# Moving the memory-value transfers ahead of a unit's values, and halving the dummy products of block 0

## The chip, the cores and the metric

The kernel runs on one core of one Trainium2 chip. The metric is the device time of one launch in microseconds (us). A core has five engines with their own instruction queues that run in program order: TensorE (PE in the profile, its weight loads PEld), VectorE (DVE), ScalarE (ACT), GpSimd (POOL) and SyncE (SP). In this kernel SP does nothing but issue DMA transfers, one after another.

## The reference, cut to what matters

Chunked attention with memory slots, then two multi-layer perceptrons on its output (3072 tokens of width 512):

```python
for c in range(nc):                      # chunks of 32 queries, per batch and head
    k_full = concat([mem_k, k_ctx])      # 8 memory keys and a window of 16 + 32 + 8
    v_full = concat([mem_v, v_ctx])
    a = softmax(scale * q_c @ k_full.T)
    out[:, :, c_start:c_end] = a @ v_full
x = out as (tokens, 512)
h = max(max(x @ w1, x @ w2), x @ w3);  x = h @ w_out        # first perceptron
h = x @ w_in;  g = where(h >= 1, h, where(h <= -1, 0, (h + 1) ** 2 / 4))
out = g @ w_out2                                             # second perceptron
```

Four batches, 8 heads, 768 positions, 8 memory slots, head width 64.

## The kernel before, in words

Attention is cut into 24 units of 128 queries, all heads at once; six units (UPB) make one batch, so units 0, 6, 12 and 18 begin a batch. Of a unit `u` the steps are: `s` scores on PE (line 379), `mx`, `ex`, `n` softmax on DVE and ACT (393, 394, 398, 402 to 405), `a` transpose of the probabilities on PE (411), `ca` copy to `aT` (415), `o` product with the values on PE (427), `cx` and `dx` split of the result into a rounded half `xh` (ACT, 437) and a rest `xl` (DVE, 441). The output product `o` of unit `u` is issued at the start of unit `u+1`, just ahead of that unit's scores.

The values of a unit lie in a tile `vw` of 128 rows: two halves of 64, each with 8 rows of memory values and 56 rows of the window, for four chunks. From unit 5 on there is one buffer. `load_v` (`lv`, line 266) fills the window rows with eight transfers from HBM. `fill_mv` (`mv`, line 255) fills the memory rows with two transfers from the small tile `mv`, once in each batch; `load_mv` (`lm`, line 248) brings that tile from HBM one batch ahead. Every transfer is issued by SP, and `mv` and `lv` of unit `u` both have to wait until `o` of unit `u-1` has read `vw`.

Tokens form six blocks of 512 (four units). Block 0 follows an order written out by hand, the string `PLAN`: attention of the first nine units, preparation of the weights (`f`, `wa` to `ws`) and the first perceptron's products for block 0 (`l`, `lt`, `lh`, `m`). A word `d3`, `d6` or `d7` in it is a call of `warm`: four products of the identity with itself into a bank that nobody reads (line 1012). Nothing on another engine waits for them; they stand in PE's queue in their places.

From then on a generator `steps(u)` yields six steps for each unit, and one step is issued beside each group of twelve or twenty-four 512-column products of the first perceptron (lines 500 to 502, the copy and maxima at 533 and 535, the split at 517 and 519). Step 1 is `o, s, cx, mx, dx, ex`; step 2 `n, lv`; step 3 transposes of keys and queries for later units by DVE (`fk` 356 and 357, `fq` 364) and the making of a list of their transfers, which `feed` then issues a few at a time (line 941); step 4 `a, ca`; step 5, until now, `mv`; step 6 `lm`. The steps of `PLAN` reach into unit 8, so that of the batch beginnings only units 12 and 18 go through the generator.

The same loop prepares the second perceptron's weights, by part of a unit (`round_step`): a fetch of 1 MB in two transfers (120 or 122), conversion on ACT and DVE (135 to 162, 176 to 179) and stores to HBM (949 to 953, 955 and 956). They share the SP queue with the units' values, in program order.

Of the kernel before, what the change touches and what calls it, by code (L numbers as in the profile page):

```python
# [37 lines left out]


PLAN = """  # L40
d3 lk1 d3 lmem0 d3 d3 lk0 d3 lm0 d3 d3 lq0 lv1 tk1 mem0 ck1 tk0 d3 ck0 ek1 tq0 lk2 kw0 d3 mv2 d3 d3
cq0 lq1 lk3 s0 mv0 mx0 lq2 tk2 mv1 d3 ck2 ek2 lk4 tq1 ex0 lv0 d3 cq1 n0 tk3 kw1 d3 ck3 s1 ek3 a0 kw2
mx1 tq2 lq3 tk4 cq2 f0 ck4 f1 s2 ex1 lk5 f2 d3 ek4 mx2 d3 f3 kw3 d3 lq4 lv2 ca0 n1 tq3 ex2 o0 cq3 n2
a1 cx0 s3 ca1 d7 dx0 wa0 mx3 o1 wr0 tk5 wc0 a2 cx1 d7 d7 ca2 d7 ex3 d7 dx1 ck5 d7 d7 ek5 wd0 d3 kw4
d3 n3 wa1 tq4 f4 d3 cq4 lv3 wc1 wr1 s4 wh0 o2 kw5 wd1 a3 d7 cx2 d7 ws0 f5 wh1 d7 lq5 d7 f6 dx2 ca3
d7 f7 mx4 lk7 o3 lv4 ws1 ex4 d7 cx3 d7 n4 d7 wa2 d6 tq5 wr2 dx3 a4 d6 wc2 cq5 ca4 s5 l0 wa3 wd2 wr3
mx5 f9 l1 f8 wh2 lv5 wc3 ex5 lt0 o4 n5 l2 cx4 lt1 ws2 lq7 a5 lq6 wd3 ca5 l3 lm1 wa4 dx4 lk6 f11 lt2
wr4 f10 wc4 l4 lh2 lt3 wh3 wd4 tq7 o5 cq7 ws3 f13 wh4 f12 tk6 mv6 l5 cx5 ws4 lk8 ck6 lv6 dx5 wa5 lt4
tq6 lt5 wr5 m0 wc5 cq6 lh5 wa6 l6 wd5 wr6 wc6 lq8 f14 wh5 f15 tk7 l7 lt6 lk9 ck7 ws5 ek7 kw6 wd6 l8
lt7 f16 wh6 f17 ws6 s6 lt8 wa7 m1 mx6 wr7 wc7 lh8 ex6 tq8 l9 cq8 wa8 wd7 m2 wr8 wc8 f18 f19 lt9 wh7  # L50
l10 wd8 ws7 f21 wh8 f20 n6 tk8 l11 ck8 ek8 lt10 kw7 ws8 wa9 tk9 lt11 l12 wr9 wc9 ck9 wa10 a6 lh11
wd9 l13 ek9 wr10 f22 f23 wc10 ca6 lt12 m3 wh9 wd10 o6 ws9 wh10 s7 lt13 cx6 lv7 ws10 wa11 l14 mx7
wr11 kw8 dx6 l15 lq10 lt14 ex7 lk10 wc11 lk11 lh14 lm2 lq9 l16 lt15 wd11 m4 n7 wh11 ws11 a7 lt16 l17
ca7 o7 lt17 lh17 s8 cx7 dx7 m5 mx8 ex8 f24 f25 f26 f27
""".split()

ON_DVE = """
# [8 lines left out]
def attention_then_two_mlps(ctx, tc, q, k, v, mem_k, mem_v, w1, w2, w3, w_mid, w_in, w_out, out):  # L66
# [8 lines left out]
    UPB = S // P  # L75
# [375 lines left out]
    def steps(u):  # L451
        old = u + 1 < TRIO0
        late = not old and u % 3 == 2
        if u == UB:
            yield [("s", u), ("mx", u), ("ex", u)]
        else:
            yield [("o", u - 1), ("s", u), ("cx", u - 1), ("mx", u), ("dx", u - 1), ("ex", u)]
        m = [("n", u), ("lv", u)]
        if old:
            v = [("tk", u + 2), ("ck", u + 2), ("ek", u + 2)] if u + 2 < TRIO0 else []  # L460
            v += [("lk", u + 4)] if u + 4 < TRIO0 else []
            yield m + v + [("kw", u + 1)]
            v = [("tq", u + 1), ("cq", u + 1)]
            v += [("lq", u + 3)] if u + 3 < TRIO0 else []
        else:
            yield m
            v = [("fk", u + 1)] * (not late)
        if u + 2 >= TRIO0:
            v += [("fq", u + 2)]
        if u == TRIO0 - 3 or u >= TRIO0 - 2 and u % 2 == 0:  # L470
            v += [("gq", u // 2 + 2)]
        if u >= TRIO0 - 2 and u % 3 == 1:
            v += [("gk", u // 3 + 1)]
        yield v
        yield [("a", u), ("ca", u)]
        new = u % UPB == 0
        yield [("mv", u)] * new + [("fk", u + 1)] * late
        yield [("lm", u // UPB + 1)] if new else []
        if u == NU - 1:
            yield [("o", u), ("cx", u), ("dx", u)]  # L480
# [3 lines left out]
    def run(kind, i):  # L484
# [3 lines left out]
        elif kind in WEIGHTS or i < NU:  # L488
            parts[kind](i)

    todo = [s for u in range(UB, NU) for s in steps(u)]
    todo.reverse()

# [386 lines left out]
    def last_evict(p):  # L880

        for i in range(2):
# [10 lines left out]
            nc.sync.dma_start(out=out[r0:r0 + 2 * P, HK:].rearrange("(t p) d -> p t d", p=P), in_=o)  # L893

    def pair_l4(p, steps):

        last = p + 1 == NB // 2
# [79 lines left out]
    with tc.manual_schedule(engines={ENG.PE, ENG.DVE, ENG.Activation, ENG.Pool, ENG.SP}):  # L977
# [56 lines left out]
        for j in range(1, NB):  # L1034
            for f in range(K1):
                l2 = [(slot_l2, *((j, f - 1) if f else (j - 1, K1 - 1)))] if j > 1 or f else []
# [154 lines left out]
```

## Time and profile before

| | |
|---|---|
| median of 3 runs | 979.41 us (979.38 to 980.14) |
| the profiled execution | 980.73 us, of which 979.0 us are the span of its instructions |
| PE busy | 952.9 us, 97% of the span |
| DVE, ACT, POOL busy | 72%, 55%, 35% |
| chain that ended last | PE 92%, DVE 3%, DMA 1%, SP's queue 1%, unexplained issue 1% |
| granted clock of TensorE, mean | 0.987 of full speed |

The span is the time from the first to the last instruction of one profiled execution. The granted clock is the share of TensorE's full clock (2.4 GHz) that the chip allowed; its lower level, 0.50, is 1.2 GHz. "issue" in the chain and among the waits is time in which an engine waited for nothing that the profile can name.

### The profile page before, as it was taken

To read this page: it belongs to the slowest core of one execution; us is meant where nothing else is said; L and a number is where in the kernel's file an instruction comes from. 1 tells how busy PE (TensorE), PEld (TensorE's weight loads), DVE (VectorE), ACT (ScalarE), POOL (GpSimd) and SP (SyncE) were. 2 spreads that over 40 slices of the span, in tenths; PEclk is the share of its full clock that TensorE was granted. 3 is DMA by queue.
4 is the path that set the end of the run, shared out by engine and by line. 5 is a ranking of instruction groups with operands and counts; after the bars stand their busy time and mean duration, and the time that the engine had idled before them with its cause. 6 is when DMAs were issued, how large, how long until landed. Compare 5 with 4: busy or idle time off the path is not lost.

```text
span 979.0 us, 19063 instructions
## 1 busy us (share of the span) xinstructions
PE 952.9 (97%) x7166; PEld 784.7 (80%) x7166; DVE 704.9 (72%) x1001; ACT 541.3 (55%) x972; POOL 339.0 (35%) x330
## 2 busy tenths in 40 slices
PE   7899999997999989999999999999999999999998
PEld 6788877886888868888888888888888888888886
DVE  2899947584776757762427777998777998777855
ACT  4766644342334223232338777776777776776763
POOL 0000002221221011111456665555655554665552
PEclk8999999998999989999999999999999999999999
DMA  7796546657677567435224226534225734323723
GB/s 173 214 230 198 159 130 159 161 146 196 183 216 191 139 167 213 148 100 188 75 72 141 85 83 224 178 109 103 92 76 153 267 113 97 87 87 97 258 65 64
DMA packets 242779, 142.81 MB, mean 146 GB/s; under 512 B 174464, under 2 KB 210176, under 8 KB 242688
## 3 DMA queue, kind: packets, MB, share of 16 engines
q1 hardware_dynamic: 242688, 141.60, 50.7%
q8 instruction: 56, 0.92, 0.4%
q14 instruction: 35, 0.29, 0.1%
HBM read 109.71 MB, written 31.46 MB: 144 GB/s over the span
## 4 chain that ended last, share of the span: by engine, by line
PE 92%; DVE 3%; DMA 1%; SPq 1%; issue 1%; ACT 1%; POOL 0%; POOLq 0%; ACTq 0%; DVEq 0%
PE psums L500 29%; PE psums L502 28%; PE psums L501 28%; PE psums L427 3%; PE psums L379 2%; PE psums L411 1%; DMA kq<-in_q_dram 1%; PE psums L1012 0%; PE psums L305 0%; PE psums L274 0%; DVE c L151 0%; SPq L941 0%; DMA vw<-mv 0%; SPq L255 0%; DVE lo L205 0%
## 5 line engine op out<-in xcount | busy, mean ns | idle before, releaser
L519 POOL TENSOR_TENSOR hl_a<-t,hh_a 128x512 fp32r<-128x512 f32 x30 | 41.4, 1380 | 398.7 <-ACT hh_a L517 387.8
L500 PE MATMUL psums<-xh,hi 128*128 128x512 f32 x432 | 173.4, 401 | 0.0
L502 PE MATMUL psums<-xh,lo 128*128 128x512 f32 x432 | 169.6, 392 | 0.0
L501 PE MATMUL psums<-xl,hi 128*128 128x512 f32 x432 | 169.3, 392 | 0.2 <-DVE xl L441 0.2
L810 POOL TENSOR_TENSOR hb<-h,hb 128x512 fp32r<-128x512 f32 x72 | 99.4, 1381 | 92.6 <-PE psums L502 59.8
L802 ACT CAST hb<-h 128x512 fp32r<-128x512 f32 x144 | 88.8, 622 | 48.1 <-PE psums L501 46.5
L535 DVE TENSOR_TENSOR t<-psums,t 128x512 f32<-128x512 f32 x72 | 49.5, 687 | 69.8 <-PE psums L502 69.8
L502 PEld LDWEIGHTS psums<-xh,lo 128*128 128x128 f32 x432 | 81.7, 189 | 18.5 <-DVE lo L205 0.9
L630 POOL TENSOR_TENSOR hb<-ra,hb 128x256 fp32r<-128x256 f32 x96 | 75.2, 796 | 58.9 <-ACT hb L629 55.6
L500 PEld LDWEIGHTS psums<-xh,hi 128*128 128x128 f32 x432 | 81.8, 189 | 16.8 <-issue 0.3
L501 PEld LDWEIGHTS psums<-xl,hi 128*128 128x128 f32 x432 | 82.0, 190 | 16.5 <-DVE xl L441 0.6
L694 ACT ACTIVATE psums<-h 128x512 f32<-128x512 f32 x96 | 57.9, 603 | 60.4 <-DVE h L780 24.2
L502 PE MATMUL psums<-t,hb 128*128 128x512 f32 x192 | 74.8, 390 | 0.0
L501 PE MATMUL psums<-t,hb 128*128 128x512 f32 x192 | 74.7, 389 | 0.0
L500 PE MATMUL psums<-t,hb 128*128 128x512 f32 x192 | 74.7, 389 | 0.0
L630 POOL TENSOR_TENSOR hb<-rb,hb 128x256 fp32r<-128x256 f32 x72 | 55.4, 775 | 39.5 <-ACT hb L629 39.5
L808 DVE TENSOR_TENSOR hb<-psums,hb 128x512 fp32r<-128x512 f32 x66 | 44.9, 680 | 24.8 <-PE psums L502 20.6
L500 PE MATMUL psums<-hh_a,hi 128*128 128x512 f32 x144 | 57.4, 399 | 1.3 <-ACT xh L437 1.3
L437 ACT CAST xh<-psums 128x512 fp32r<-128x512 f32 x24 | 14.0, 585 | 79.8 <-PE psums L379 50.9
L695 ACT ACTIVATE psums<-psums 128x512 f32<-128x512 f32 x96 | 55.9, 582 | 3.1
L833 DVE TENSOR_TENSOR h<-h,h 128x1024 f32<-128x1024 f32 (+1 forms) x42 | 56.5, 1368 | 0.0
L502 PE MATMUL psums<-hh_a,lo 128*128 128x512 f32 x144 | 56.2, 390 | 0.0
(145 smaller groups left out, 2301.0 us busy)
## 6 DMA issues: line engine op xcount, KB each, us to landing
t<-td SPq DMA_DIRECT2D x15, 1024.0 KB
ra<-cd SPq DMA_DIRECT2D x24, 512.0 KB
st<-in_moe_w_out_dram SPq DMA_DIRECT2D x22, 512.0 KB
st<-in_moe_w_dram SPq DMA_DIRECT2D x18, 512.0 KB
vw<-in_v_dram SPq DMA_DIRECT2D x152, 56.0 KB
st<-in_moe_w_in_dram SPq DMA_DIRECT2D x16, 512.0 KB
h<-yd SPq DMA_DIRECT2D x12, 512.0 KB
rb<-cd SPq DMA_DIRECT2D x24, 256.0 KB
```

The costliest lines, as they stand in the source:

```text
L500: nc.tensor.matmul(out, whi, xhi, start=first, stop=False)
L501: nc.tensor.matmul(out, whi, xlo, start=False, stop=False)
L502: nc.tensor.matmul(out, wlo, xhi, start=False, stop=last)
L519: e.tensor_tensor(out=lo, in0=h, in1=hi.bitcast(F32), op=ALU.subtract)
L535: nc.vector.tensor_tensor(out=cur["t", j, f], in0=s, in1=cur["t", j, f], op=ALU.max)
L630: nc.gpsimd.tensor_tensor(out=c[:, 1], in0=t, in1=c[:, 0].bitcast(F32), op=ALU.subtract)
L694: nc.scalar.activation(out=a, in_=x, func=AF.Relu, bias=0.5, scale=0.5)
L695: nc.scalar.activation(out=a, in_=a, func=AF.Square)
L802: nc.scalar.copy(out=hi, in_=x)
L808: nc.vector.tensor_tensor(out=lo, in0=y, in1=hi.bitcast(F32), op=ALU.subtract)
L810: nc.gpsimd.tensor_tensor(out=lo, in0=x, in1=hi.bitcast(F32), op=ALU.subtract)
L833: nc.vector.tensor_tensor(out=x, in0=y, in1=z, op=op)
```

## The change

Two edits. In `steps`, the word `mv` of a unit that begins a batch moves from step 5 to step 2, between `n` and `lv`: its two transfers are now issued ahead of the eight of `lv` and not after the transfers that `feed` and the weight stores issue in steps 3 and 4. Nothing else of the generator changes; for units 12 and 18 the issue order on SP differs, and on no other engine.

In `PLAN`, 19 of the 37 words `d` are left out, with four products each: 76 of 148. What stays: five before the first key transpose, one before `s0` (`kw0 d3 mv2 cq0 lq1 lk3 s0`), one after `s2`, six around `ca2 ex3 dx1 ck5 ek5`, three after `a3`, two after `o3`. All other words keep their order. Among those left out are the ones between `tk0` and `tq0`, between `tk2` and `tq1`, `tq1` and `tk3`, `tk3` and `s1`, two of three after `s2`, the one between `s3` and `o1`, and the one between `a4` and `s5`.

```diff
 PLAN = """
-d3 lk1 d3 lmem0 d3 d3 lk0 d3 lm0 d3 d3 lq0 lv1 tk1 mem0 ck1 tk0 d3 ck0 ek1 tq0 lk2 kw0 d3 mv2 d3 d3
-cq0 lq1 lk3 s0 mv0 mx0 lq2 tk2 mv1 d3 ck2 ek2 lk4 tq1 ex0 lv0 d3 cq1 n0 tk3 kw1 d3 ck3 s1 ek3 a0 kw2
-mx1 tq2 lq3 tk4 cq2 f0 ck4 f1 s2 ex1 lk5 f2 d3 ek4 mx2 d3 f3 kw3 d3 lq4 lv2 ca0 n1 tq3 ex2 o0 cq3 n2
-a1 cx0 s3 ca1 d7 dx0 wa0 mx3 o1 wr0 tk5 wc0 a2 cx1 d7 d7 ca2 d7 ex3 d7 dx1 ck5 d7 d7 ek5 wd0 d3 kw4
...
+d3 lk1 d3 lmem0 d3 d3 lk0 d3 lm0 lq0 lv1 tk1 mem0 ck1 tk0 ck0 ek1 tq0 lk2 kw0 d3 mv2 cq0 lq1 lk3 s0
+mv0 mx0 lq2 tk2 mv1 ck2 ek2 lk4 tq1 ex0 lv0 cq1 n0 tk3 kw1 ck3 s1 ek3 a0 kw2 mx1 tq2 lq3 tk4 cq2 f0
+ck4 f1 s2 ex1 lk5 f2 d3 ek4 mx2 f3 kw3 lq4 lv2 ca0 n1 tq3 ex2 o0 cq3 n2 a1 cx0 s3 ca1 dx0 wa0 mx3 o1
+wr0 tk5 wc0 a2 cx1 d7 d7 ca2 d7 ex3 d7 dx1 ck5 d7 d7 ek5 wd0 kw4 n3 wa1 tq4 f4 cq4 lv3 wc1 wr1 s4
...
-        m = [("n", u), ("lv", u)]
+        m = [("n", u)] + [("mv", u)] * (u % UPB == 0) + [("lv", u)]
...
-        yield [("mv", u)] * new + [("fk", u + 1)] * late
+        yield [("fk", u + 1)] * late
```

## Rows read from the trace of the kernel before

**Rows 1.** The page: busy us of each engine, share, instructions

```profile
PE 952.9 (97%) x7166; PEld 784.7 (80%) x7166; DVE 704.9 (72%) x1001; ACT 541.3 (55%) x972; POOL 339.0 (35%) x330
```

**Rows 2.** Waits of PE, 60 to 450 us: total us, times, longest

```profile
PE psums L427 <- issue: 9.2, 2, 4.7
PE psums L500 <- ACT xh L437: 1.3, 1, 1.3
```

**Rows 3.** Chain that ended last, 205 to 235 us: start us, us, what

```profile
223.76 2.48 DMA vw<-mv
226.29 1.93 PE psums L427 x62
```

**Rows 4.** The same chain over the whole span, units 12 to 19

```profile
212.49 0.44 PE psums L411 x4
...
239.47 0.44 PE psums L411 x4
...
258.35 0.44 PE psums L411 x4
...
266.98 1.06 PE psums L427 x64
...
333.90 0.44 PE psums L411 x4
...
359.86 0.44 PE psums L411 x4
```

**Rows 5.** Timeline of SP: start us, us, line, transfer, count

```profile
207.81 5.52 SPq L266 DMA_DIRECT2D vw<-in_v_dram  x8
...
222.97 1.47 SPq L255 DMA_DIRECT2D vw<-mv  x2
...
232.24 4.47 SPq L266 DMA_DIRECT2D vw<-in_v_dram  x8
238.71 4.92 SPq L941 DMA_DIRECT2D kq<-in_k_dram  x10
...
251.21 0.89 SPq L120 DMA_DIRECT2D st<-in_moe_w_out_dram  x2
...
254.59 6.22 SPq L266 DMA_DIRECT2D vw<-in_v_dram  x8
...
332.72 4.87 SPq L266 DMA_DIRECT2D vw<-in_v_dram  x8
...
343.50 1.68 SPq L255 DMA_DIRECT2D vw<-mv  x2
```

**Rows 6.** Timelines of ACT and DVE in unit 14

```profile
259.31 1.12 ACT L135 ACTIVATE c<-st 128x1024 f32<-128x1024 f32 x1
...
263.67 0.70 DVE L356 STREAM_TRANSPOSE kw<-kq 128x512 f32<-128x512 f32 x1
```

**Rows 7.** Groups of PE by line, 0 to 50.6 us: busy us, mean ns, idle before

```profile
L1012 PE MATMUL psums<-ident 128*128 128x256 bf16 x148 | 20.9, 296 | 1.4 <-POOL ident masks.py:199 1.4
```

**Rows 8.** Chain that ended last, 0 to 60 us

```profile
16.84 0.85 PE psums L1012 x4
...
23.48 1.42 PE psums L1012 x12
...
26.18 1.93 issue
...
48.13 0.70 DVE p L405
...
49.53 0.44 PE psums L1012 x4
```

**Rows 9.** By stretch: us, busy us of PE, PEld, DVE, ACT, POOL; granted clock; DMA

```profile
28.00:32.00 4.00, 3.89 (x103) 2.96 (x104) 2.34 (x5) 2.50 (x4) 0.00 (x0) 0.57 1.05 273
...
44.00:48.00 4.00, 3.39 (x85) 3.00 (x84) 3.90 (x7) 2.47 (x4) 0.00 (x0) 1.00 1.06 316
...
120.00:140.00 20.00, 18.71 (x210) 15.16 (x209) 8.62 (x14) 8.90 (x16) 0.00 (x0) 1.00 0.47 155
```

More of the change, by code (lines that the diff above doesn't have):

```diff
@@ L40 @@
 PLAN = """
-d3 lk1 d3 lmem0 d3 d3 lk0 d3 lm0 d3 d3 lq0 lv1 tk1 mem0 ck1 tk0 d3 ck0 ek1 tq0 lk2 kw0 d3 mv2 d3 d3
-cq0 lq1 lk3 s0 mv0 mx0 lq2 tk2 mv1 d3 ck2 ek2 lk4 tq1 ex0 lv0 d3 cq1 n0 tk3 kw1 d3 ck3 s1 ek3 a0 kw2
-mx1 tq2 lq3 tk4 cq2 f0 ck4 f1 s2 ex1 lk5 f2 d3 ek4 mx2 d3 f3 kw3 d3 lq4 lv2 ca0 n1 tq3 ex2 o0 cq3 n2
-a1 cx0 s3 ca1 d7 dx0 wa0 mx3 o1 wr0 tk5 wc0 a2 cx1 d7 d7 ca2 d7 ex3 d7 dx1 ck5 d7 d7 ek5 wd0 d3 kw4
-d3 n3 wa1 tq4 f4 d3 cq4 lv3 wc1 wr1 s4 wh0 o2 kw5 wd1 a3 d7 cx2 d7 ws0 f5 wh1 d7 lq5 d7 f6 dx2 ca3
@@ L46 @@
[L46 to L54, printed above, removed]
+d3 lk1 d3 lmem0 d3 d3 lk0 d3 lm0 lq0 lv1 tk1 mem0 ck1 tk0 ck0 ek1 tq0 lk2 kw0 d3 mv2 cq0 lq1 lk3 s0
+mv0 mx0 lq2 tk2 mv1 ck2 ek2 lk4 tq1 ex0 lv0 cq1 n0 tk3 kw1 ck3 s1 ek3 a0 kw2 mx1 tq2 lq3 tk4 cq2 f0
@@ new lines @@
+ck4 f1 s2 ex1 lk5 f2 d3 ek4 mx2 f3 kw3 lq4 lv2 ca0 n1 tq3 ex2 o0 cq3 n2 a1 cx0 s3 ca1 dx0 wa0 mx3 o1
+wr0 tk5 wc0 a2 cx1 d7 d7 ca2 d7 ex3 d7 dx1 ck5 d7 d7 ek5 wd0 kw4 n3 wa1 tq4 f4 cq4 lv3 wc1 wr1 s4
+wh0 o2 kw5 wd1 a3 d7 cx2 d7 ws0 f5 wh1 d7 lq5 f6 dx2 ca3 f7 mx4 lk7 o3 lv4 ws1 ex4 d7 cx3 d7 n4 wa2
+tq5 wr2 dx3 a4 wc2 cq5 ca4 s5 l0 wa3 wd2 wr3 mx5 f9 l1 f8 wh2 lv5 wc3 ex5 lt0 o4 n5 l2 cx4 lt1 ws2
+lq7 a5 lq6 wd3 ca5 l3 lm1 wa4 dx4 lk6 f11 lt2 wr4 f10 wc4 l4 lh2 lt3 wh3 wd4 tq7 o5 cq7 ws3 f13 wh4
@@ new lines @@
+f12 tk6 mv6 l5 cx5 ws4 lk8 ck6 lv6 dx5 wa5 lt4 tq6 lt5 wr5 m0 wc5 cq6 lh5 wa6 l6 wd5 wr6 wc6 lq8 f14
+wh5 f15 tk7 l7 lt6 lk9 ck7 ws5 ek7 kw6 wd6 l8 lt7 f16 wh6 f17 ws6 s6 lt8 wa7 m1 mx6 wr7 wc7 lh8 ex6
+tq8 l9 cq8 wa8 wd7 m2 wr8 wc8 f18 f19 lt9 wh7 l10 wd8 ws7 f21 wh8 f20 n6 tk8 l11 ck8 ek8 lt10 kw7
+ws8 wa9 tk9 lt11 l12 wr9 wc9 ck9 wa10 a6 lh11 wd9 l13 ek9 wr10 f22 f23 wc10 ca6 lt12 m3 wh9 wd10 o6
+ws9 wh10 s7 lt13 cx6 lv7 ws10 wa11 l14 mx7 wr11 kw8 dx6 l15 lq10 lt14 ex7 lk10 wc11 lk11 lh14 lm2
@@ L55 @@
+lq9 l16 lt15 wd11 m4 n7 wh11 ws11 a7 lt16 l17 ca7 o7 lt17 lh17 s8 cx7 dx7 m5 mx8 ex8 f24 f25 f26 f27
 """.split()
```

## The prediction

> **What bounds the kernel now.** I read the page first: PE is busy 97% of the span [rows 1], so a change counts only where it takes away PE time or a wait of PE. Next the waits of PE. Between block 0's beginning and the end of attention nearly all of them belong to one line, the output product at 427: 9.2 us in two waits [rows 2], which the profile cannot name itself ("issue"). Then the chain of waits around the first one. It says what released PE: a transfer `vw<-mv`, issued at 223.76, landed 2.48 later, at 226.24, and the product runs from 226.29 [rows 3]. That is `o` of unit 12, waiting for the memory rows of its value tile. SP's timeline says why they came late: their two issues stand at 222.97, behind feeds and weight stores, while the unit's eight value transfers were issued at 207.81 [rows 5]. Unit 18 repeats the pattern: values at 332.72, memory rows at 343.50 [rows 5].
>
> What a stall costs in all I take from the period of the units, measured from one transpose `a` to the next: undisturbed 258.35 - 239.47 = 18.88 us; over the first stall 239.47 - 212.49 = 26.98; over the second 359.86 - 333.90 = 25.96 [rows 4]. The excess is 8.10 and 7.08, 15.18 together, of which 9.2 are idle; the other 6.0, about 3.0 for each, is PE running slowly afterwards (the product took 1.93 [rows 3] where an ordinary one takes 1.06 [rows 4]).
>
> **The move, part by part.** It adds and removes no instruction. Two issues of 1.47 us in all (1.68 in unit 18) [rows 5] go ahead of the eight value issues.
>
> *Unit 12.* An ordinary `o` starts 266.98 - 258.35 = 8.63 us after `a` [rows 4], so `o` of unit 12 is due at 212.49 + 8.63 = 221.12. Its values' last issue ends at 207.81 + 5.52 + 1.47 = 214.80 at the latest. From the end of an issue to landing I take 226.24 - (222.97 + 1.47) = 1.8 [rows 3, 5]. That gives 216.6: 4.5 us to spare, and the memory rows are earlier still. *Unit 18:* due at 333.90 + 8.63 = 342.53; values issued by 332.72 + 4.87 + 1.68 = 339.27, landed 341.1: 1.4 to spare. Both stalls should go, and with them the slow stretch behind each: -15.18. What waits behind the moved issues on SP (feeds, stores) is later by at most 1.5 to 1.7 us, until the place that the pair left; from there SP is where it was.
>
> *What is late next.* PE reaches units 13 and 14 8.10 us sooner, but SP does not. It is almost never idle from 207.81 to the end of unit 14's values at 254.59 + 6.22 = 260.81 [rows 5]. Unit 13: `o` due at 239.47 - 8.10 + 8.63 = 240.0; values end at 232.24 + 4.47 = 236.71 as before, landed 238.5: hidden, by 1.5. Unit 14: `o` due at 266.98 - 8.10 = 258.88. If SP gains nothing, the values land at 260.81 + 1.8 = 262.6, 3.7 late. SP gains at least the hole between 236.71 and 238.71 [rows 5], which is a wait for DVE's transposes to free the key buffer, and those come with PE, 8 us sooner. With 2.0 gained they land at 260.6, 1.7 late; the pair's old place may give back another half. Bounds 0 (SP gains more than I can see) and 3.7; I take 1.5, near the row of the hole.
>
> In the same unit the fetch at 251.21 moves only those 2 us, while ACT's conversion at 259.31, which needs it, is due at 251.2. That conversion delays DVE, and the key transpose at 263.67 stands behind it [rows 5, 6]. How late the conversion gets depends on the fetch's landing, of which the rows give bounds alone: 1.8 after its issue ends at 250.1 (0.7 late) and 2.0 before the conversion ran, at 257.3 (6.1 late). The key transposes (two of 0.70, to 265.1) were done 2.9 us before the scores that need them, at 266.98 + 1.06 = 268.04 [rows 4, 6]. With the 1.5 already counted, 4.4 us of delay stay hidden, the middle of the bounds (3.4) among them: I add 0, with 1.7 as the other end.
>
> A second stall of 1.5 us could also drop the clock. Against that stands a wait of 1.3 us for `xh` [rows 2]; it is the 1.29 us that PE is not busy in 120 to 140 us, where the clock stayed at 1.00 [rows 9]. I take no drop.
>
> **The dummy products.** 76 of 148 go. At the full clock four of them take 0.44 [rows 8], so 8.4 us of PE time leave the first 50 us (20.9 for all [rows 7]). Little of that is on the path. The chain holds none before 16.84: up to there it runs through SP and DMA. Then it holds two groups of 0.85 (one stands in rows 8), two thirds of 1.42 at 23.48, both ahead of a 1.93 issue stall at 26.18, and 0.44 at 49.53 [rows 8]; one more group lies in the slow stretch after the stall. From about 35 to 48.8 the chain is on ACT and DVE, and late in it DVE is busy 3.90 of 4.00 us [rows 9]; the transpose `a` of unit 4 waits for DVE's softmax, which ends at 48.83 [rows 8], whatever PE did before. Behind it only the last group is a plain saving, 0.44, of which the ACT copy of unit 5's queries, just ahead of its scores, leaves about 0.2. The earlier groups, 0.85 + 0.85 + 0.95 = 2.65, help only as far as they let DVE begin that busy stretch sooner; the stall at 26.18 and ACT's copies stand between. Bounds 0 and 2.65; I count none, since a stall that PE itself did not cause is the nearest row.
>
> What the dummies hid: without them PE idles between the small attention products, and the clock can fall. The rows show that it does in this stretch: after the 1.93 us of waiting at 26.18 [rows 8] the granted clock in 28 to 32 is 0.57, a mix of 0.50 and 1.00, while 44 to 48, with dummies, is at 1.00 [rows 9]. If it is at 0.50 when block 0's first large product starts, at about 50.5, the price is what the slow stretches of units 12 and 18 cost, 3.0. At half clock earlier than that, PE's small products have DVE's busy stretch to hide behind. Eighteen of the 37 groups remain, among them eleven between 34 and 47 us, so I take 0 here and keep 3.0 for the range. The Trainium skill, TensorE: Matmul & The Clock Gate, in its section on what is actually happening, says that the low clock is the default and that activity releases it; its section on oscillation says that waits between bursts of products bring it back. By that rule the half that is left out would cost the 3.0 and the sum would be three less; the trace agrees with the rule at 28 to 32 us but does not show whether the remaining half is enough.
>
> **The sum.** -15.18 (two stalls) + 1.5 (unit 14's values) + 0 (conversion) - 0.2 (last dummy group) + 0 (clock) = -13.9. The profiled execution took 980.73 for a span of 979.0 and would take 966.8. The median of the runs, 979.41, is 1.32 below it, so the median becomes 979.41 - 13.9 = 965.5. After 450 us nothing changes: PE runs without waits, and what it feeds shifts with it.
>
> **The rivals.** (A) As summed: 961.6 to 968, chance 0.62. (B) SP takes back more: unit 14's values are 3.7 late, and the idle time halves the clock (3.0): 6.7 given back in place of 1.5, 970.7; the conversion's 1.7 would lie within the same wait. For it speaks that SP has hardly a hole for 50 us; against it, that one hole is a wait that vanishes. The milder form, 1.5 and the clock, is 968.5. Chance 0.15. (C) The clock is at half at block 0's first large products: +3.0, 968.5; for and against as above; chance 0.13. (D) The change doesn't do what it says: what held `o` of units 12 and 18 was something behind the memory rows and as late, and the wait keeps its length under another name: about 979.2. Against it stands the landing at 226.24 and the start 0.05 later [rows 3]; for it, that the profile itself calls most of the waiting "issue" [rows 2]. Chance 0.05. (E) Slower: the clock stays at 0.50 well into block 0. Each slow stretch of units 12 and 18 cost about 3.0 us before the clock was back [rows 2, 4]; the 13.9 are used up only by nearly five such stretches on end, and from there it decides: six give 979.41 - 13.9 + 18 = 983.5. Nothing in the trace comes near. Chance 0.02. (F) The dummies' 2.65 and no give-back: 979.41 - 15.18 - 2.65 = 961.6; chance 0.03.
>
> **The numbers.** This kernel's runs tell about 0.2% (2 us) from no change. Faster by more than that are A, B, C and F: 0.93; within it D: 0.05; slower E: 0.02. The range goes from F's 961.5 to 972.0, past B: all but D, E and a remainder.
>
> **What would show it right or wrong.** Right: no wait at line 427 near 221 or 335; the transposes of units 12 and 13, and 18 and 19, 18.9 apart; a wait of 1 to 2 us at 427 near 259 with the clock at 1.00; transpose `a` of unit 4 still released by DVE near 48.8; clock 1.00 from 50 us on. Wrong: a clock of 0.50 at 50 to 54 us (C); a wait above 2 us near 259 and 0.50 behind it, or waits in unit 15 too (B); waits of 4 us left at 427 in units 12 and 18 (D); block 0's first large product two or more us sooner than 50.7 (F).

## The result, and the profile after

The changed kernel took 969.03 us (median of 4 runs, 967.93 to 969.68), the kernel before 979.39 (median of 4, 977.88 to 980.14) beside it on the same chip: ratio 0.9895 [0.9878, 0.9912], 10.4 us faster. The prediction was 965.5 with a range of 961.5 to 972.0, so the median lies inside it. The profiled execution took 968.48 us for a span of 966.7, so against the profile of before the span is 12.3 us shorter, where 13.9 were forecast.

In the code after, line numbers are one lower than before (`o` is 426, `a` 410, the scores 378, the first perceptron's products 499 to 501, the copy `t` 532, the conversion 134, the fetch 119).

The page after, busy us of each engine, answers to [rows 1]:

```profile
PE 945.5 (98%) x7090; PEld 777.7 (80%) x7090; DVE 705.2 (73%) x1001; ACT 542.2 (56%) x972; POOL 339.5 (35%) x330
```

PE has its 76 dummy instructions less and nothing else changed in count. Waits of PE after, 60 to 450 us, answer to [rows 2]: total us, times, longest.

```profile
PE psums L499 <- ACT t L532: 3.3, 1, 3.3
...
```

The two waits of `o`, 9.2 us together, are gone, and so is the one of 1.3 for `xh`. Below what the fence shows come 0.8 and 0.2. A wait stands there that [rows 2] did not have: a large product waits 3.3 us for ACT's copy `t`. The chain that ended last, transposes `a` of units 12 to 16 and the stretch of that wait, answers to [rows 4]:

```profile
210.23 0.44 PE psums L410 x4
...
229.11 0.44 PE psums L410 x4
...
256.62 1.06 PE psums L426 x64
...
266.87 0.44 PE psums L410 x4
...
270.90 3.58 DMA vw<-in_v_dram
274.48 1.13 ACT st L138
275.60 0.47 ACT t L532
276.12 0.61 PE psums L499
276.73 0.43 PE psums L500
...
291.00 0.44 PE psums L410 x4
```

Unit 12 now takes 229.11 - 210.23 = 18.88 us, an undisturbed period, where it took 26.98: 8.10 gained. Unit 15 takes 291.00 - 266.87 = 24.13, 5.25 more than undisturbed: 3.3 of waiting, and the rest at half clock (granted 0.59 and 0.56 in 276 to 278 and 278 to 280 us), for the products behind the wait take 0.43 us each instead of the usual 0.23. The chain puts a value transfer ahead of ACT's second conversion step (274.48). That is an inference from times that coincide: the step reads and writes `st` alone, and in ACT's timeline below the wait stands ahead of the first step, where the landing of the fetch ends it. Further down the same chain unit 18 is undisturbed too:

```profile
328.76 0.44 PE psums L410 x4
...
347.64 0.44 PE psums L410 x4
```

18.88 again, where it was 25.96: 7.08 gained. So the shifts of `a` against the profile of before are -2.26 from block 0 and the wait for `xh` (210.23 against 212.49), -10.36 behind unit 12, -5.13 behind unit 15 (291.00 against 296.13 for unit 16), -12.22 behind unit 18, and nothing afterwards.

SP's timeline after shows why ACT was late in unit 15; it answers to [rows 5]. Columns: start us, us, line, transfer, count.

```profile
204.60 1.46 SPq L254 DMA_DIRECT2D vw<-mv  x2
206.10 5.39 SPq L265 DMA_DIRECT2D vw<-in_v_dram  x8
...
229.04 4.74 SPq L265 DMA_DIRECT2D vw<-in_v_dram  x8
233.88 4.96 SPq L940 DMA_DIRECT2D kq<-in_k_dram  x10
...
249.47 4.98 SPq L265 DMA_DIRECT2D vw<-in_v_dram  x8
...
264.05 3.93 SPq L352 DMA_DIRECT2D kT<-in_q_dram  x6
268.09 0.87 SPq L119 DMA_DIRECT2D st<-in_moe_w_out_dram  x2
```

And ACT's timeline after, units 14 (as [rows 6]) and 15; in brackets the idle time ahead and what ended it:

```profile
251.44 1.12 ACT L134 ACTIVATE c<-st 128x1024 f32<-128x1024 f32 x1 [2.39 <-DMA st<-in_moe_w_out_dram]
...
267.35 0.59 ACT L414 COPY aT<-psums 128x512 f32<-128x512 f32 x1 [3.52 <-PE psums L410]
267.83 0.62 ACT L516 CAST hh_a<-t 128x512 fp32r<-128x512 f32 x1
273.45 1.13 ACT L134 ACTIVATE c<-st 128x1024 f32<-128x1024 f32 x1 [5.00 <-DMA st<-in_moe_w_out_dram]
274.47 1.14 ACT L138 ACTIVATE st<-st 128x1024 uint32<-128x1024 uint32 x1
275.50 0.57 ACT L532 COPY t<-psums 128x512 f32<-128x512 f32 x1
```

The fetch of unit 15's weights is issued at 268.09, behind the flush of the transposed queries (264.05), with no gap on SP. ACT reaches the conversion right behind 267.83, stands still for 5.00 us until `st` has landed, and the copy `t`, which needs nothing of that fetch, is queued behind the two conversion steps. PE's large products take turns in two PSUM banks, and it needs the one that `t` empties.

Of block 0, the windows by stretch answer to [rows 9] (us, busy us of PE, PEld, DVE, ACT, POOL; granted clock; DMA share, GB/s):

```profile
44.00:48.00 4.00, 3.43 (x19) 2.13 (x17) 3.90 (x7) 3.69 (x5) 0.00 (x0) 0.53 1.06 327
48.00:52.00 4.00, 4.00 (x74) 3.27 (x74) 3.84 (x6) 3.37 (x4) 0.00 (x0) 0.61 0.85 162
52.00:56.00 4.00, 4.00 (x41) 3.10 (x39) 3.86 (x7) 1.62 (x3) 0.00 (x0) 1.00 0.85 276
```

and the chain that ended last, from 41 us on, answers to [rows 8]:

```profile
41.05 4.82 DMA kq<-in_q_dram
...
45.91 1.11 PE psums L304 x4
47.03 1.02 PE psums L410 x4
...
49.16 0.72 PE psums L499
```

Transpose `a` of unit 4 starts at 47.03 here, where the softmax that it waited for in [rows 8] ended at 48.83, and no longer waits for it: PE comes to it straight from the transposes of unit 5's queries (line 304), which waited for those queries until 45.87. The clock fell to 0.50 at about 44.2 us and was back from about 51.

### The profile page after: what moved, and what is told of

It reads as the page before. It is cut to its first block, busy times and chain, and to the rows that moved or that the text cites. A ratio compares the mean times of both kernels' runs of the same rounds, so it can differ in the third digit from the quotient of the medians.

```text
span 966.7 us, 18906 instructions
## 1 busy us (share of the span) xinstructions
PE 945.5 (98%) x7090; PEld 777.7 (80%) x7090; DVE 705.2 (73%) x1001; ACT 542.2 (56%) x972; POOL 339.5 (35%) x330
## 4 chain that ended last, share of the span: by engine, by line
PE 93%; DVE 2%; DMA 2%; SPq 1%; ACT 1%; issue 1%; POOL 0%; POOLq 0%; DVEq 0%; ACTq 0%
PE psums L499 29%; PE psums L501 28%; PE psums L500 28%; PE psums L426 2%; PE psums L378 2%; PE psums L410 1%; PE psums L273 1%; DMA kq<-in_k_dram 1%; DMA kq<-in_q_dram 0%; PE psums L304 0%; PE psums L1011 0%; DMA vw<-in_v_dram 0%; SPq L360 0%; SPq L265 0%; SPq L940 0%
## 5 line engine op out<-in xcount | busy, mean ns | idle before, releaser
L500 PE MATMUL psums<-hl_a,hi 128*128 128x512 f32 x144 | 56.2, 390 | 0.0
```

The lines of the kernel that those rows point to most:

```text
L500: nc.tensor.matmul(out, whi, xlo, start=False, stop=False)
```

## The experiments

Each ratio is against the kernel before, run beside it on the same chip; those medians of before were 977.52 (the first four kernels), 977.34 (e5 to e8) and 975.94 (e9 to e12).

| | median us | ratio, interval |
|---|---|---|
| e1 the move alone | 967.16 | 0.9890 [0.9873, 0.9906] |
| e2 the halved dummies alone | 974.96 | 0.9967 [0.9951, 0.9983] |
| e3 both, conversion of unit 15 a step later | 965.34 | 0.9869 [0.9846, 0.9892] |
| e4 both, three of the late dummy groups put back | 965.35 | 0.9864 [0.9841, 0.9886] |
| e6 the change again | 967.29 | 0.9911 [0.9883, 0.9939] |
| e7 both, stores and fetch ahead of the feeds in a step | 968.94 | 0.9920 [0.9891, 0.9948] |
| e9 both, fetch right behind the stores | 976.27 | 1.0005 [0.9983, 1.0027] |
| e10 as e4, conversion a step later in all units | 963.22 | 0.9869 [0.9839, 0.9899] |
| e11 as e4, fetch earlier and conversion later | 978.32 | 1.0034 [1.0010, 1.0057] |
| e12 the move, no dummy at all | 962.31 | 0.9866 [0.9831, 0.9901] |

e5 (before, 979.17) and e8 (967.84) ran once each, for their traces. By these intervals e3, e4, e10 and e12 can't be told from each other, and e3 and e4 touch those of the change (0.9895 and, in e6, 0.9911): what single waits are worth is read from the traces.

**The two edits alone.** e1 has the edit of `steps`, e2 the new `PLAN`, nothing else.

```diff
 # e1
-        m = [("n", u), ("lv", u)]
+        m = [("n", u)] + [("mv", u)] * (u % UPB == 0) + [("lv", u)]
-        yield [("mv", u)] * new + [("fk", u + 1)] * late
+        yield [("fk", u + 1)] * late
 # e2: only the words "d" of PLAN that the change leaves out
```

> The move alone, all 148 dummy products kept. Theory: the two edits add up, and the move brings the two stalls (15.2 us) less what unit 15 gives back where ACT's conversion waits for the weight fetch (5.2 in the profile of the changed kernel): about 10 faster than before, with a wait of PE of about 3 us for the copy t in unit 15. Rival: the give-back comes only because the halved dummies let PE run 2 us further ahead of SP; then unit 15 shows less than half of that wait, and the move alone brings 13 or more.

> Only the dummy products halved, the move undone. Theory: DVE's busy stretch in block 0 begins about 2 us sooner, and after the first 140 us the trace stands about 2.2 us ahead of before; the stalls of units 12 and 18 remain, since their end is set by SP's queue, but the first of them begins sooner, so that part of the 2.2 is lost to it if SP does not move: 0 to 2.2 faster. Rival (my prediction): 0.2 faster, within what can be told from none; and the 2.2 of the profile is the scatter of early DMA traffic.

e1 gains 10.36 us and e2 2.56, which add up to 12.9; the whole change gained 10.4 (and 10.1 when it was run again, e6). The 2.5 between them are no more than the intervals leave open, but the traces agree that the two take something from each other. Waits of PE in e1, 60 to 450 us:

```profile
PE psums L500 <- ACT xh L437: 1.0, 1, 1.0
...
```

The next are 0.8 and 0.2, and none is for `t`: with the old `PLAN` PE comes to unit 15 at 270.82, 3.95 later than after the change, while SP issues the fetch at 268.65, only 0.56 later. So of e1's theory the size came true and the reason did not: unit 15 gives back 0.14 us in place of 5.2, as the rival had it, and yet the gain is 10.36 and not 13. Part of that is the smaller stalls of the next paragraph: of e5's 12.6 us, 0.14 go in unit 15 and 0.64 before unit 8 (141.18 against 140.54), which leaves the 11.8 that lie between the spans of e5 and e1 (977.4 and 965.6). In e2 both waits of `o` are there (`L426 <- issue` 8.5 in two), so the dummies have nothing to do with the stalls.

**How large the stalls are: the kernel before once more (e5), and the change once more (e6), no edit.**

> The kernel before, profiled a second time. Theory: the first 60 us (small products between early transfers, with a clock that falls and rises) differ from execution to execution by some us, the two stalls of units 12 and 18 do not; so the excess of the two disturbed periods is again 8.1 and 7.1 within 0.5, and what differs between the two profiles lies before 140 us. Rival: the stalls themselves vary, which is why the median gained less than the trace shows; then one of them is shorter by 2 us or more.

> The changed kernel again, on the chip and in the rounds of the next two. Theory: the wait for the copy t in unit 15 is there again (3 us, and 5 in all with the clock); the clock at 44 to 51 us may stand at either level, since a kernel with the same dummies showed 1.00 there. Rival: the wait in unit 15 was chance, and its loss comes out under 2 us.

ACT's copies of `a` for units 12, 13 and then 18, 19 in e5 (start, us):

```profile
214.06 0.58 ACT L415 COPY aT<-psums 128x512 f32<-128x512 f32 x1 [2.52 <-PE psums L411]
236.88 0.58 ACT L415 COPY aT<-psums 128x512 f32<-128x512 f32 x1 [5.75 <-PE psums L411]
...
331.29 0.58 ACT L415 COPY aT<-psums 128x512 f32<-128x512 f32 x1 [2.52 <-PE psums L411]
358.85 0.59 ACT L415 COPY aT<-psums 128x512 f32<-128x512 f32 x1 [7.69 <-PE psums L411]
```

Unit 12 exceeds the 18.88 of an undisturbed unit by 3.94 here and unit 18 by 8.68: 12.6 together, against 15.18 in the profile that the prediction used. In e2, which has the same stalls, it is 232.34 - 208.92 - 18.88 = 4.54 and 354.55 - 327.07 - 18.88 = 8.60, 13.1 together. The first number of the sum was thus one draw, and the largest of three, as e5's rival had it. e6 repeats the loss of unit 15 (5.17 in place of 5.25, the wait for `t` 3.3 again), so that one is no accident; it adds 1.65 in unit 19, with another wait for `t`, of 1.4.

**Is it the order within the step?** e8 keeps the move to step 2 but issues the memory rows behind the eight value transfers.

```diff
-        m = [("n", u)] + [("mv", u)] * (u % UPB == 0) + [("lv", u)]
+        m = [("n", u), ("lv", u)] + [("mv", u)] * (u % UPB == 0)
```

> The changed kernel with the memory rows behind the unit's eight value transfers, still in step 2. Theory: what counts is that they no longer stand behind feeds and stores; they land by 217 in unit 12 and 341 in unit 18, before the product is due: no wait, periods of 18.9 us as in the changed kernel. Rival: the order within the step matters, and a wait of 1 us or more is left in unit 18, where my margin was 1.4 us.

The stalls are gone as well; a wait of 0.3 for `vw<-mv` is left at line 426, in unit 18, well under the 1 us of the rival. What counts is the distance to the feeds and stores of steps 3 and 4, not which of the two goes first.

**Conversion later.** In e3 ACT's conversion (`"a"`) of unit 15 alone is issued one step later, behind the copies `t` of the step where it blocked; in e10 that of every unit, together with three dummy groups put back as in e4.

```diff
 # e3
+                if done == 45:
+                    acts.remove("a")
+                if done == 46:
+                    acts.insert(0, "a")
 # e10
-    BY_PART = "", "p", "", "out a", "in in", "b"
+    BY_PART = "", "p", "", "out", "a in in", "b"
-                round_step(BY_PART[part].split() + (["a"] if s == 1 else []))
+                round_step(BY_PART[part].split())
```

> The changed kernel, with the conversion that waits 5 us for its fetch in unit 15 put one step (3.1 us of products) later, behind the copy t that PE needs. Theory (the conversion blocks ACT's queue, and PE waits for the copy behind it, not for the weights): the wait of 3.3 us for t goes, and the slow clock behind it: 3 to 5.2 us faster than the changed kernel. Rival (PE was held by DVE or by a bank that the late fetch holds in another way): the wait stays at 3 us under another name, no change.

> The version with the last three dummy groups back, and the conversion one step later in every unit. Theory: no wait for t above 1 us in units 15, 19 and 20, the gain of the move is kept whole: about 12 to 14 faster than before. Rival: the later conversion makes the stores or DVE's combining late, and waits of PE turn up elsewhere; no better than the version with the dummies alone.

ACT's timeline of e3 in unit 15:

```profile
266.52 0.59 ACT L414 COPY aT<-psums 128x512 f32<-128x512 f32 x1 [5.10 <-PE psums L410]
...
269.32 0.59 ACT L532 COPY t<-psums 128x512 f32<-128x512 f32 x1 [1.70 <-PE psums L501]
270.43 1.12 ACT L134 ACTIVATE c<-st 128x1024 f32<-128x1024 f32 x1 [0.52 <-DMA st<-in_moe_w_out_dram]
```

The copy runs ahead of the conversion, as soon as PE has the product; no wait at `t` is left in unit 15, and one of 0.8 for `xl` of DVE has come up there, probably since the later conversion delays DVE. From unit 15 to 16 that is 286.53 - 266.52 = 20.01 between ACT's copies of `a`, 1.13 over the undisturbed 18.88 and not 5.25: 4.1 gained there. e10 has no wait for `t` left from 60 to 450 us; one for `xl` (1.3, at 204 us) is the largest. Its unit 15 loses 0.45, where e4, with the same dummies and the conversion in its old place, loses 1.90. Both ratios are 0.9869, and e4's is 0.9864: the traces of unit 15 show what the later conversion does, the medians don't show it by themselves.

**Fetch earlier on SP.** If the conversion waits for the fetch, the fetch could come first. e7 has stores and fetch issued ahead of the feeds of the same step, e9 the fetch in the step of the stores, e11 that and the later conversion.

```diff
 # e7
-                feed((5, 6, 4, 6, 5, 1)[part])
                 round_step(BY_PART[part].split() + (["a"] if s == 1 else []))
+                feed((5, 6, 4, 6, 5, 1)[part])
 # e9: as e7, and
-    BY_PART = "", "p", "", "out a", "in in", "b"
+    BY_PART = "", "p", "", "out a in in", "", "b"
 # e11: round_step ahead of feed and without the "a" of s == 1, dummies as e4, and
+    BY_PART = "", "p", "", "out in in", "a", "b"
```

> The changed kernel with the weight stores and fetches issued in each step ahead of the feed transfers instead of behind them. Theory (SP's order makes the fetch late, not the transfer itself): the fetch of unit 14 is issued 2 to 5 us sooner against PE, ACT's wait of 5.0 us in unit 15 shrinks below 2, PE's wait for t goes: 3 to 5 faster than the changed kernel. Rival (DMA bandwidth or the landing of the stores sets it): the fetch waits for the landing of the stores anyway, gain under 1; or the feeds come late instead and DVE waits for keys and queries: slower.

> The changed kernel with the weight fetch issued right behind the weight stores, both ahead of the feed transfers of that step (the earlier version moved it only within its own step, where a flush of feeds still stood ahead of it). Theory (SP's order makes the fetch late): in unit 14 the fetch is issued 3 to 5 us sooner against PE, ACT's wait in unit 15 falls below 2, PE's wait for t goes, 3 to 5 faster than the changed kernel. Rival (the landing of the stores, or DMA bandwidth): the fetch waits for the stores' landing and gains under 1; with feeds late, DVE waits for keys or queries.

> Fetch early and conversion late together, last three dummy groups back. Theory: the same as the better of the two, with more slack, ACT's waits for fetches under 1 us in all units; 12 to 15 faster than before. Rival: feeds become late; waits of DVE for keys or queries move into PE.

e7 did not do what it was made for: the stores go out at 256.84, but twelve feeds and flushes still stand between them and the fetch, which is issued at 268.99, no sooner than the 268.09 after the change. It says nothing for or against; its unit 15 loses 5.78. e9 did move the fetch, to 247.85 and 270.11, each 3.6 to 4.5 us ahead of the transpose of its unit. Waits of PE in e9, 60 to 450 us:

```profile
PE psums L426 <- DMA vw<-in_v_dram: 3.1, 12, 0.5
...
```

and its chain at units 13 to 18:

```profile
228.77 0.44 PE psums L410 x4
...
251.50 0.44 PE psums L410 x4
...
274.61 0.44 PE psums L410 x4
...
294.82 0.44 PE psums L410 x4
...
313.70 0.44 PE psums L410 x4
...
338.80 0.44 PE psums L410 x4
```

No wait for `t`, but now the values come late: 251.50 - 228.77 = 22.73, 274.61 - 251.50 = 23.11, 294.82 - 274.61 = 20.21 and 338.80 - 313.70 = 25.10 exceed 18.88 by 3.85, 4.23, 1.33 and 6.22, 15.6 in all (3.1 of it in the waits above; over units 13, 14 and 17 the granted clock is down to 0.92, 0.93 and 0.86), so that the stalls are back under another name and the ratio is 1.0005. Why the values are late, SP's own waits show (200 to 345 us) and its timeline:

```profile
SPq L119 <- DMA rd<-st: 12.1, 4, 4.0
...
```

```profile
243.59 0.82 SPq L952 DMA_DIRECT2D rd<-st  x1
247.85 0.83 SPq L119 DMA_DIRECT2D st<-in_moe_w_out_dram  x2
248.72 8.89 SPq L940 DMA_DIRECT2D kq<-in_k_dram  x16
257.71 3.87 SPq L265 DMA_DIRECT2D vw<-in_v_dram  x8
```

Pulled to right behind the weight stores, the fetch stands in SP's queue until these have landed (it fills a tile `st` that they read), and everything behind it stands too: the feeds, and then the values, which start at 257.71 for the product due at 251.50 + 8.63 = 260.13. That is the landing of the stores that the rival on record named. In the changed kernel feeds stand between the stores and the fetches at 223.91, 246.15 and 268.09, which wait 0.6 us together for the landing. e11 shows the same (12.2 in 4 on SP, 5.1 in 16 at the values). So an earlier place for the fetch made the values late; whether another place on SP has room was not run.

**The dummies.** e4 puts back three groups (12 products: one more behind `o3`, one ahead of `tq5`, one between `a4` and `s5`); e12 takes out all that the change had left.

```diff
 # e4
-... lk7 o3 lv4 ws1 ex4 d7 cx3 d7 n4 wa2 tq5 wr2 dx3 a4 wc2 cq5 ca4 s5
+... lk7 o3 lv4 ws1 ex4 d7 cx3 d7 n4 d7 wa2 d6 tq5 wr2 dx3 a4 d6 wc2 cq5 ca4 s5
 # e12: PLAN of the change without any word "d"
```

> The changed kernel with the last three groups of dummies put back (two behind the output product of unit 3, one between a4 and s5: 12 products). Theory: they hold the clock; the granted clock at 44 to 51 us stays at 1.00, the first large products of block 0 run at 0.23 us each, and block 0's second output product stands about 1 us sooner than in the changed kernel; the end gains 0 to 1, since a later wait for ACT or DVE takes some of it. Rival: the clock falls there anyway, because the waits in front of that stretch are what lowers it: 0.50 again, and the three groups cost up to 1.

> The changed kernel without any dummy product. Theory: the clock stands at 0.50 for most of the first 50 us and into block 0's first large products, PE's small products at half clock make DVE's busy stretch late; block 0's second output product comes 2 to 5 us later than in the changed kernel, and the end 1 to 4 later. Rival: the dummies never mattered, since ACT and DVE set the pace there; block 0 starts no later, and the end is the same or earlier.

Windows of e12, the kernel without dummies:

```profile
36.00:40.00 4.00, 3.01 (x75) 2.51 (x68) 3.79 (x5) 2.53 (x4) 0.00 (x0) 0.50 0.75 196
...
44.00:48.00 4.00, 3.37 (x73) 2.47 (x73) 3.83 (x8) 3.31 (x5) 0.00 (x0) 0.50 1.13 327
48.00:52.00 4.00, 4.00 (x17) 3.29 (x18) 3.88 (x6) 2.96 (x3) 0.00 (x0) 0.93 0.49 90
```

PE runs at half clock for a dozen microseconds, and it costs nothing that shows, as the rival had it: DVE is busy 3.8 to 4.0 of every 4.00 us from 36 to 48, and the transpose `a` of unit 4 starts at 45.75, earlier than the 46.94 of the change (PE's timeline; 47.03 in the chain) and the 48.87 of before. At `a` of unit 8 this execution was 4.04 ahead of the profile of before. e4 kept the clock at 1.00 from 33 us on, as its theory had it, and was 3.25 ahead there; e11, with the same groups, had 1.00 from 44 us on and e10 from 45. e12 and e10 have the lowest medians, 962.31 and 963.22, on a chip where the kernel before had its lowest too.

## Why the prediction was nearly right, point by point

**The move.** Right in mechanism, and in size for the execution it was taken from: -8.10 and -7.08 forecast, 8.10 and 7.08 found between the two profiles. e1, e2 and e8 show that it is the move that does it; rival D, the wait under another name, falls. What was mis-sized is the step from that profile to the median: 15.18 is one execution's, and others of the same stalls gave 12.6 (e5) and 13.1 (e2).

**What is late next.** This step failed. It looked for the give-back at `o` of unit 14 and took 1.5; the product started at 256.62, 8.63 behind its transpose like any other, so nothing was lost. The step had held that SP gains 2.0 by the hole and is otherwise where it was. Unit 14's values were issued by 249.47 + 4.98 = 254.45 in place of 260.81, 6.4 sooner: block 0 brought SP 1.7 (206.10 against 207.81), the pair's old place 1.5 more (229.04 against 232.24), the hole 1.6 (233.88 against 238.71), and the rest came with the feeds ahead of unit 14 and in its own issue (4.98 in place of 6.22). By the 1.8 from issue to landing they had 0.4 us to spare.

**The conversion, counted at 0.** This is the term that was mis-sized: 5.25 us. The step followed the late fetch to ACT, but then only to DVE's key transposes, and only in unit 14. There the fetch moved 5.1 and not 2 (246.15 against 251.21), and the conversion did wait (2.39) and cost nothing. One unit on, PE had gained 10.37 us (266.87 against 277.24) and the fetch 5.60 (268.09 against 273.69). The step left out what is queued behind the waiting instruction on its own engine: the copy `t`, with which PE's next products are held up. How far the fetch is ahead of ACT's copy of `a` in unit 15 orders all the runs with the move that kept the conversion in its place, but for e9, whose fetch was moved:

| | fetch issue minus copy of `a`, us | ACT waits for the fetch | unit 15 over 18.88 |
|---|---|---|---|
| e12 | 262.57 - 265.57 = -3.00 | no | 0.11 |
| e1 | 268.65 - 271.29 = -2.64 | no | 0.14 |
| e8 | 267.15 - 268.25 = -1.10 | 3.26 | 1.90 |
| e4 | 265.52 - 266.41 = -0.89 | 3.27 | 1.90 |
| e6 | 266.77 - 266.26 = 0.51 | 4.95 | 5.17 |
| after | 268.09 - 267.35 = 0.74 | 5.00 | 5.25 |
| e7 | 268.99 - 267.89 = 1.10 | 5.57 | 5.78 |

(In e7 the profile lets value transfers, issued right behind the fetch, end ACT's wait.) With the stalls still there, in before, e2 and e5, the fetch is 4.0 to 4.1 ahead and unit 15 loses 0.01 to 0.34. Of ACT's wait some 1.7 us are hidden (5.00 against PE's 3.3), the rest is PE's. In the change, e6 and e7, where PE waits 3.3 to 3.9, the granted clock falls to 0.50 behind the wait and comes on top; in e4 and e8, where it waits 1.6, the clock stays at 1.00. e3 and e10, which take the copy out from behind the conversion, are the test of it, and e9 and e11, which move the fetch instead, pay for it with the values. In kind this was rival B, SP taking back more, at another engine than where B had it, and 5.25 is within its 6.7; waits in unit 15 were on record as a sign of B.

**The dummies, counted at -0.2.** Mis-sized too: e2's median measures 2.6 us, 1.7 to 4.8 by its interval. The transpose `a` of unit 4 starts at 44.90 to 47.85 us in the seven profiles with the new `PLAN` (the change, e2, e3, e6 to e9; mean 46.9) and at 48.87, 50.09 and 49.95 in the three with the old one (before, e1, e5; mean 49.6): 2.7 sooner, the 2.65 that were kept as the other bound, and not 0. At unit 8 it is 135.90 to 138.13 (mean 136.9) against 139.49, 141.18 and 140.54 (mean 140.4), 3.5 sooner. Of that 1.0 is a wait for `xh` between units 7 and 8 (0.8 to 1.3 us), which the three with the old `PLAN` have and the seven do not; the prediction had not counted on its going, and why it goes is not shown. That the groups between 16 and 26 us stood ahead of DVE's busy stretch after all is the likely reason for the rest, but argued, not shown. The issue stall in which they were to vanish is no fixed place either. The chain before has it at 26.18, ahead of `o` of unit 0 [rows 8]; the chain after has 1.90 us at 26.26, in the middle of the scores of unit 3. In e5, the kernel before again, it is 2.29 at 29.91, inside another `o`; in e6, the change again, PE has no such wait above 0.9.

**The clock.** Counted at 0 with 3.0 as rival C. C came, in the profile after and in three more of the seven with the new `PLAN` (e6, e7, e8): the first large products run at 0.50. It did not come in e2, e3 and e9, nor in any of the three with the old `PLAN`, nor where the last three groups were put back (e4, e10, e11). But where it came it cost less than 3.0: from the first large product to block 0's first `o` there are 6.6 to 7.0 us in place of 5.7, so 0.9 to 1.4. In the profile after the small products just ahead took 0.7 more as well (from `a` of unit 4 to that `o` 8.70 in all, against 7.54 before, of which 0.44 were a dummy group).

**The sum.** In the two profiles -15.18 - 2.26 + 5.25 = -12.2, which is the 12.3 of the span. As forecast it was -15.18 - 0.2 + 1.5. The two errors go against each other, by +3.75 and -2.06, so that the median lies in the range is in part luck. Of the signs on record for a right prediction, the periods of 18.9 and the missing waits at `o` of units 12 and 18 came; the wait near 259, the release of unit 4's `a` by DVE and the full clock from 50 us did not. The median moved by 10.4 and not 12.3 because the profiled execution of before was 1.3 slower than the median of its runs (980.73 against 979.39) and that of after 0.6 faster (968.48 against 969.03). The runs of before spread by some 2 to 10 us, and its stalls are smaller in e2 and e5 than in the profile that the sum was taken from; that this is the whole of the difference is not shown.

**Still open:** why SP is 5 us ahead of the profile after at unit 12 in e12, the kernel without dummies (the fetch goes out at 198.08 in place of 202.92, and waits there for the landing of the weight stores in both, 2.1 and 3.8 us), which spares e12 the wait of unit 15; and whether no dummies and the later conversion together are faster than either, which was not run.

## What to carry to other kernels

When a stall is removed, PE gains on every queue that the stall had let catch up: subtract the gain from each of them over several units, not only the first, and at each late arrival ask what is queued behind the instruction that waits on its own engine, needed or not. Where an in-order engine serves both a critical eviction and a background job fed by DMA, put the background job behind the eviction. Moving its transfer forward in an in-order issue queue helps only if the transfer can start there: here it had to wait for its buffer, and everything behind it waited too. And a stall's size in one profile is one draw: a second profile of the same kernel would have put the first term at 12.6 and not 15.2.

## What the hardware did that was not expected

The granted clock at the end of block 0 differs between executions of the same order of instructions: 0.50 from 44.2 to 51 us in the profile after, from 47 to 50.4 in e6, and 1.00 all along in e3. Windows of e3:

```profile
44.00:48.00 4.00, 1.80 (x25) 1.26 (x31) 3.86 (x8) 3.24 (x5) 0.00 (x0) 1.00 0.97 292
48.00:52.00 4.00, 4.00 (x79) 3.33 (x80) 3.84 (x6) 1.21 (x2) 0.00 (x0) 1.00 0.91 210
```

PE is busy 2.43 of 4.00 us in 40 to 44, just ahead, in e3 as in the profile after. In 44 to 48 it is busy 1.80 in e3, at full clock, and 3.43 after the change, at 0.53. The Trainium skill, TensorE: Matmul & The Clock Gate, section "What's actually happening", says of a kernel's first products that the point at which the clock rises varies from run to run, depending on where the first product falls. The runs here agree in kind, in the middle of a kernel and for a fall. By the rule of that section of the Trainium skill that the low clock is the default and activity lifts it, e12 should get its clock back with the first large products, and it does (0.93 in 48 to 52, from 0.50).

An idle time of PE that the profile cannot name ("issue") stands in block 0 in most of these executions, at other places and of other lengths in the same kernel: 1.93 us at 26.18 and 2.29 at 29.91 in the two profiles of before. What it is, the profile does not name.
